# Chunk 0 of a chunked retention in whole 128-position blocks, and a new order of the early work

## The chip, the core and the metric

The kernel runs on one core of a Trainium2 chip. The core has a matrix engine (TensorE; in the profile PE for its matmuls, PEld for its weight loads), VectorE (DVE), ScalarE (ACT), GpSimd (POOL) and SyncE (SP), which issues the transfers. Each engine works through its own instructions in the order in which they were issued, and waits on semaphores for the others. Matmuls write to PSUM; DVE and ACT read it from there. The metric is the device time of one execution in microseconds.

## The reference

A retention layer with a state that decays for each head, and after it a feed-forward block with SiLU. B = 4, H = 8, S = 768, D = 64; the feed-forward block has 3072 tokens, 512 inputs and 2048 hidden units.

```python
gamma = 1.0 - 2.0 ** (-5.0 - np.arange(H))
for t in range(S):
    state = gamma * state + k[:, :, t] (outer) v[:, :, t]
    y[:, :, t] = scale * (q[:, :, t] @ state)
x = y.transpose(0, 2, 1, 3).reshape(B * S, H * D)
h = x @ w_in
out = (h * sigmoid(h)) @ w_out
```

The weights come as 64-bit floating-point words, which the kernel turns into 32-bit ones itself.

## The kernel before, in words

**Units.** The sequence is cut into 6 chunks of 128 positions. A unit n is one chunk c and one batch b, n = 4c + b, so units 0 to 3 are chunk 0 and units 4 to 7 chunk 1. Within a unit each chunk is split again into two halves of 64 positions (index o), and the 8 heads are four pairs (a) of two (j).

**Steps of a unit.** The early part of the kernel, up to line 1121, is an order written out by hand for all five engines, as calls of short functions:

- T(n), or TK(n) and TQ(n) (line 470): k and q are transposed on PE, four transposes each (line 485), and copied by ACT to kt and qt (line 486).
- K(n) scales k by its decay on DVE (line 424); KA(n) does the same on ACT in eight pieces (line 949).
- SC(n): the sums of k times v of both halves (line 514, 32 records on PE), then the scores k times q within each half (line 524, 32 records).
- A(n), three calls: the scores are masked with decay on DVE (line 532); mid, the state between the halves, is made (in chunk 0 by an ACT copy, line 538, later by a DVE addition, line 540); the state after the unit is a DVE addition (line 544).
- Q(n): q is scaled by its decay gq on DVE (line 429); in chunk 0 only the second half.
- YS(n), Y0(n), YB(n): the output, as masked scores times v (32 records, line 572), then states times q in two parts. Between the parts stands a fence: a memset on POOL (line 406) that waits for the first part, and for which the second waits.
- X(n), four calls: ACT copies the output (line 619), ACT makes its high part (line 643), DVE the rest (line 646) and the third part (line 649). The three parts of a chunk, for all four batches, are the right operand xt of the products.
- next_chunk() multiplies gq by the decay of a chunk on ACT (line 379).

**Weights.** W(i) takes slice i of w_in one step on, of eleven: two ACT passes and four DVE passes turn the words into 32-bit numbers, ACT and DVE then split these in three parts. load_w(i) issues the slice's three transfers, load(name, n) one of 256 KB.

**Products.** PP(n, i) is a third of product n (line 930; n = 16 is chunk 1, slice 0): four matmuls of 512 columns each. CL(n) closes a product: ACT copy, DVE subtraction, ACT SiLU. After the early order come pair (1, 1) and all the other products (line 744), ordered by a list, and then the second half of the feed-forward block (line 1237).

**Fillers.** fill and narrow issue matmuls of zeros into an unused or not yet written PSUM bank (lines 317 and 323). The tables FILL_T, NARROW_T, FILL_Y, NARROW_Y, FILL_FENCE and FILL_P (lines 459 to 465) say how many stand ahead of, or behind, which step.

**What sets the order.** On PE, DVE, ACT, POOL and SP the order of the early part is that of the calls; the rest of the kernel after line 1121 is ordered by hand on PE only.

Of the kernel before, what the change touches and what calls it, by code (L numbers as in the profile page):

```python
# [13 lines left out]
FP32 = mybir.dt.float32  # L14
# [20 lines left out]
def kernel(  # L35
# [39 lines left out]
    wide = moe_w_in.dtype == mybir.dt.int64  # L75

    scale = 1.0 / math.sqrt(D)
    assert math.frexp(scale)[0] == 0.5
# [95 lines left out]
    def load_w(i):  # L174
        if i >= 2 * NF:
            return
        if wide:
            t = stage.tile([128, 2 * DM], U32, tag="wf", name=f"wf_{i}")
            w_in, w_out, n = moe_w_in.bitcast(U32), moe_w_out.bitcast(U32), 256
        else:  # L180
            t = stage.tile([128, DM], FP32, tag="wf", name=f"wf_{i}")
            w_in, w_out, n = moe_w_in, moe_w_out, 128
        if i < NF:
            to = t.rearrange("p (i o f) -> o p i f", o=2, f=n)
            src = w_in[:, ts(i, n)].rearrange("(i o p) f -> o p i f", o=2, p=128)
            last[:] = [nc.sync.dma_start(out=to[0], in_=src[0]).ins]
            for j in range(2):
                nc.sync.dma_start(out=to[1, ts(j, D)], in_=src[1, ts(1 - j, D)])
        else:
            nc.sync.dma_start(out=t, in_=w_out[ts(i - NF, 128), :])  # L190
        staged[i] = t

    def convert_steps(i, out):

        t = staged.pop(i)
        if not wide:
            out.append(t)
            return
        words = t.rearrange("p (c w) -> p c w", w=2)
        lo, hi = words[:, :, 0], words[:, :, 1]  # L200
        a = conv.tile([128, DM], U32, tag="ca", name=f"ca_{i}")
        s = conv.tile([128, DM], U32, tag="cs", name=f"cs_{i}")
        r = lo if i >= NF else conv.tile([128, DM], U32, tag="cw", name=f"cw_{i}")
        with queue(evac[0] if evac else None):
            top = nc.scalar.activation(out=a.bitcast(FP32), in_=hi.bitcast(FP32), func=AF.Abs,  # L205
                                       scale=2.0 ** -3).ins
# [128 lines left out]

    lag = const.tile([128, C], FP32, tag="lag", name="lag")
    for o in range(2):
        part = lag[ts(o, D), :D]
        nc.gpsimd.iota(part, pattern=[[1, D]], base=0, channel_multiplier=-1,
                       allow_small_or_imprecise_dtypes=True)  # L340
        nc.gpsimd.affine_select(out=part, in_=part, compare_op=ALU.is_ge, fill=1.0e6,
                                base=0, pattern=[[1, D]], channel_multiplier=-1)
    decay = const.tile([128, 2, HP, D], FP32, tag="decay", name="decay")
    for j in range(2):
        for a in range(HP):
            nc.scalar.activation(out=decay[:, j, a, :], in_=lag[:, :D], func=AF.Exp,
                                 scale=float(lg[2 * a + j]))

    gk = const.tile([128, NC, H], FP32, tag="gk", name="gk")
# [8 lines left out]
    for h in range(H):  # L358
        nc.scalar.activation(out=gk[:, 0, h : h + 1], in_=pos, func=AF.Exp,
                             scale=float(-lg[h]))  # L360
        nc.gpsimd.memset(lgc[ts(h % 2, D), h // 2 : h // 2 + 1], lg[h])
    nc.gpsimd.iota(lag, pattern=[[1, C]], base=1, channel_multiplier=0,
                   allow_small_or_imprecise_dtypes=True)
    for a in range(HP):
        nc.scalar.activation(out=gq[:, a, :], in_=lag, func=AF.Exp, scale=lgc[:, a : a + 1])
# [26 lines left out]
    def banks(tag, name, n=2):  # L392
        return ps_u.tile([128, n, 512], FP32, tag=tag, name=name)
# [23 lines left out]
    def scale_k(n):  # L417
        if 0 <= n < len(units):
# [4 lines left out]
            engine = nc.gpsimd if 2 * B + 1 < n < FAR else nc.vector  # L423
            engine.tensor_tensor(out=t, in0=t, in1=g, op=ALU.mult)

    def scale_q(n):
        c, b = units[n]
        t, g = (x if c > 0 else x[:, :, D:] for x in (qt[n], gq))
        nc.vector.tensor_tensor(out=t, in0=t, in1=g, op=ALU.mult)
# [179 lines left out]
    def steps_y(n, yp):  # L609
# [5 lines left out]
        if c < LATE:  # L615
            if n == 0:
                raws.append(wpool.tile([128, LATE * B, KIN, C], FP32, tag="wq", name="ys"))
            raw = raws[0][:, n]
            nc.scalar.copy(out=raw.rearrange("p a (o t) -> p o a t", o=2), in_=yp)
# [276 lines left out]

    K, Q = scale_k, scale_q

    idle[:] = [banks("y", "idle")[:, 0]]
    narrow(idle[0], 39)  # L900
    fill(idle[0], 2)
    narrow(idle[0], 39)
    T(0), K(0)
    nc.scalar.activation(out=token, in_=lgc[:1, :1], func=AF.Silu)
    SC(0), A(0), Q(0), A(0), A(0)
    W(0), W(0), W(0), W(0), W(0)
    YA(0), YB(0), X(0)
    T(1), K(1)
    W(0)
    W(0)  # L910
    X(0), X(0)
    SC(1), A(1)
    W(0)
    A(1)
    Q(1), A(1)
    T(2), K(2)
    W(0), X(0)
    W(0), W(0)
    YA(1), SC(2)
    A(2)  # L920
    YB(1), X(1)
    A(2), Q(2), A(2)
    X(1)
    closing = {}

    made = {}
# [19 lines left out]
    def KA(n):  # L946
        t = kqv["k"][n]
        for h in range(H):
            nc.scalar.activation(out=t[:, h, :], in_=t[:, h, :], func=AF.Copy,
                                 scale=gk[:, units[n][0], h : h + 1])  # L950

    TK(3)
    TQ(3)
    K(3)
    X(1)
    X(1)
    YS(2)
    Y0(2)
    YB(2)
    X(2)  # L960
    SC(3)
    A(3)
    A(3)
    Q(3)
    A(3)
    X(2)
    W(1)
    W(1)
    X(2)
    X(2)  # L970
    YS(3)
    Y0(3)
    YB(3)
    X(3)
    X(3)
    TK(4)
    W(1)
    X(3)
    X(3)
    W(1)  # L980
    TQ(4)
    load("k",6)
    W(1)
    load_w(2)
    load("q",6)
    load("k",7)
    W(1)
    W(1)
    load("v",6)
    load("q",7)  # L990
    PP(0,0)
    KA(4)
    PP(0,1)
    W(1)
    load("k",9)
    PP(0,2)
    load("v",7)
    CL(0)
    SC(4)
    load("k",8)  # L1000
    next_chunk()
    TK(5)
    A(4)
    TQ(5)
    TK(6)
    A(4)
    Q(4)
    A(4)
    K(5)
    W(1)  # L1010
    CL(0)
    YS(4)
    load("q",8)
    W(2)
    W(2)
    W(1)
    Y0(4)
    SC(5)
    W(1)
    W(2)  # L1020
    YB(4)
    X(4)
    Q(5)
    A(5)
    CL(0)
    A(5)
    PP(1,0)
    load("q",9)
    W(2)
    W(2)  # L1030
    TQ(6)
    PP(1,1)
    W(2)
    KA(6)
    load("k",10)
    PP(1,2)
    YS(5)
    put_g(0)
    A(5)
    W(2)  # L1040
    W(2)
    Y0(5)
    W(2)
    SC(6)
    CL(1)
    CL(1)
    X(4)
    A(6)
    W(2)
    YB(5)  # L1050
    W(2)
    TK(7)
    X(4)
    A(6)
    PP(2,0)
    X(5)
    load("v",8)
    PP(2,1)
    PP(2,2)
    load("v",9)  # L1060
    A(6)
    Q(6)
    TQ(7)
    K(7)
    X(5)
    YS(6)
    load_w(3)
    CL(2)
    load("v",10)
    Y0(6)  # L1070
    SC(7)
    YB(6)
    X(6)
    load_w(4)
    A(7)
    Q(7)
    TK(8)
    TQ(8)
    A(7)
    X(6)  # L1080
    YS(7)
    Y0(7)
    CL(1)
    K(8)
    YB(7)
    A(7)
    CL(2)
    X(7)
    X(5)
    X(7)  # L1090
    TK(9)
    X(4)
    hold(masked[0])
    X(5)
    TQ(9)
    X(7)
    PP(NF,0)
    KA(9)
    SC(8)
    load("q",10)  # L1100
    X(6)
    X(7)
    X(6)
    A(8)
    put_g(0)
    next_chunk()
    PP(NF,1)
    PP(NF,2)
    CL(NF)
    load("k",11)  # L1110
    CL(2)
    CL(NF)
    A(8)
    A(8)
    CL(NF)
    put_g(0)
    Q(8)
    load("q",11)
    taken[0] = 3
    begin_w()  # L1120
    early_order.close()
    written[0] = False

# [191 lines left out]
```

## Time and profile before

| | |
|---|---|
| median of 3 runs | 611.1 us (610.76, 611.1, 611.9) |
| profiled execution | 616.74 us |
| span of it (first to last instruction) | 614.7 us |
| mean granted TensorE clock | 0.991 |
| busy: PE, PEld | 605.3 us, 499.8 us |
| busy: DVE, ACT, POOL | 396.3 us, 326.8 us, 33.4 us |
| moved by DMA | 108.89 MB, mean 177 GB/s |

How to read the rows that follow. A row of stretches has the window, its length, the busy time and the number of instructions of PE, PEld, DVE, ACT and POOL, then the granted TensorE clock, the busy share of the DMA engines and GB/s. A row of the chain of waits has its start, its length and what set the time. A row of the timeline has start, length, engine, line, operation, what it writes and reads, and in brackets the idle time before it with what ended it. A row of groups has line, engine, operation, shapes and count, then the busy time and the mean of one in ns, then idle time before. A matmul of 32-bit floats is recorded twice, once for each of its two passes, as is its weight load. The ends of matmuls are modelled.

### The profile page before, as it was taken

Reading aid. Unit: us, or ns where it says so; the run is one execution under the profiler, and the core shown is the slowest. Engines: PE = TensorE matmul, PEld = TensorE weight load, DVE = VectorE, ACT = ScalarE, POOL = GpSimd, SP = SyncE. Lnnn points to the kernel's source line nnn. Section 1 sums busy time; section 2 is a strip of 40 time slices with the busy share of each in tenths; the row PEclk is TensorE's granted clock in tenths of the full one; section 3 lists DMA queues with packets and bytes.
Section 4 is the critical chain, followed back from the end, with each engine's and each line's share of the span. In section 5 each row is a group of like instructions: output and inputs, shape, how many; then the busy total and the mean of one; then the engine's idle time right before and its main releaser. Section 6 shows DMA issues by size and latency. Waiting matters only on the chain.

```text
span 614.7 us, 13719 instructions
## 1 busy us (share of the span) xinstructions
PE 605.3 (98%) x5509; PEld 499.8 (81%) x5509; DVE 396.3 (64%) x672; ACT 326.8 (53%) x607; POOL 33.4 (5%) x89
## 2 busy tenths in 40 slices
PE   8998999999999999999999999999999999999997
PEld 6786888888888888888888888888888888888886
DVE  4885899678886667665779783735545453644632
ACT  7786877677767667776698632312221321313211
POOL 3000120100021111120000000000000000000000
PEclk9997999999999999999999999999999999999999
DMA  8995779785799699999777542523524433432301
GB/s 191 234 203 138 185 165 289 235 256 173 259 249 196 178 261 250 272 266 273 274 234 267 170 152 68 189 85 103 171 70 137 137 103 103 145 129 93 113 1 68
DMA packets 144334, 108.89 MB, mean 177 GB/s; under 512 B 101136, under 2 KB 109584, under 8 KB 144272
## 3 DMA queue, kind: packets, MB, share of 16 engines
q1 hardware_dynamic: 144272, 108.03, 62.2%
q8 instruction: 43, 0.70, 0.5%
q14 instruction: 19, 0.16, 0.1%
HBM read 66.06 MB, written 36.70 MB: 167 GB/s over the span
## 4 chain that ended last, share of the span: by engine, by line
PE 96%; ACT 1%; DMA 1%; issue 1%; SPq 1%; DVE 0%; DVEq 0%; POOL 0%; ACTq 0%; POOLq 0%
PE ha L744 28%; PE o L1237 21%; PE oa L1237 14%; PE hb L744 14%; PE ob L1237 7%; PE y L572 4%; PE sc L514 2%; PE sc L524 2%; PE ha L930 1%; DMA wf<-in_moe_w_in_dram 1%; PE kp L485 1%; PE qp L485 1%; PE hb L930 0%; PE o L1257 0%; PE kp L495 0%
## 5 line engine op out<-in xcount | busy, mean ns | idle before, releaser
L744 PE MATMUL ha<-xt,wi 128*128 128x512 f32 x736 | 184.2, 392 | 0.0
L744 PEld LDWEIGHTS ha<-xt,wi 128*128 128x128 f32 x736 | 136.7, 188 | 29.1
L1237 PE MATMUL o<-wo,gs 128*128 128x512 f32 x564 | 143.1, 389 | 0.0
L832 ACT ACTIVATE gs<-gr 128x512 fp32r<-128x512 f32 x96 | 53.2, 621 | 139.0 <-issue 137.9
L1237 PEld LDWEIGHTS o<-wo,gs 128*128 128x128 f32 x564 | 105.9, 188 | 22.0
L834 DVE TENSOR_TENSOR gs<-gr,gs 128x512 fp32r<-128x512 f32 x96 | 62.2, 686 | 94.2 <-ACT gs L832 94.2
L1237 PE MATMUL oa<-wo,gs 128*128 128x512 f32 x376 | 115.8, 389 | 0.0
L744 PE MATMUL hb<-xt,wi 128*128 128x512 f32 x368 | 98.3, 389 | 0.0
L772 DVE TENSOR_TENSOR g<-g,hb 128x512 f32<-128x512 f32 x87 | 59.6, 685 | 53.6 <-ACT g L767 39.6
L1237 PEld LDWEIGHTS oa<-wo,gs 128*128 128x128 f32 x376 | 70.6, 188 | 14.6
L744 PEld LDWEIGHTS hb<-xt,wi 128*128 128x128 f32 x368 | 69.1, 188 | 14.3
L1237 PE MATMUL ob<-wo,gs 128*128 128x512 f32 x188 | 73.1, 389 | 0.0
L777 ACT ACTIVATE g<-g 128x512 f32<-128x512 f32 x87 | 54.7, 628 | 33.2 <-DVE g L772 33.1
L767 ACT ACTIVATE g<-ha 128x512 f32<-128x512 f32 x87 | 51.7, 594 | 27.1 <-PE ha L744 18.9
L835 DVE SCALAR_TENSOR_TENSOR gs<-gs 128x512 fp32r<-128x512 f32 x96 | 62.1, 684 | 0.1
L1237 PEld LDWEIGHTS ob<-wo,gs 128*128 128x128 f32 x188 | 35.3, 188 | 7.4
L205 ACT ACTIVATE ca<-wf 128x512 f32<-128x512 f32 x32 | 21.5, 670 | 7.0 <-DVE cs L218 4.2
L532 DVE TENSOR_TENSOR am<-sc,decay 128x512 f32<-128x512 f32 x24 | 16.5, 689 | 12.2 <-PE sc L524 12.1
L1278 ACT ACTIVATE o<-o 128x512 f32<-128x512 f32 x10 | 6.0, 600 | 33.4 <-PE o L1237 33.0
L218 DVE SCALAR_TENSOR_TENSOR cs<-ca,cs 128x512 uint32<-128x512 uint32 x32 | 23.2, 724 | 0.9
L572 PE MATMUL y<-qt,mid 64*64 64x64 f32 x376 | 20.0, 224 | 2.3 <-issue 2.3
L649 DVE SCALAR_TENSOR_TENSOR xt<-xt 128x512 fp32r<-128x512 f32 x28 | 19.7, 714 | 0.6
(136 smaller groups left out, 614.0 us busy)
## 6 DMA issues: line engine op xcount, KB each, us to landing
gr<-gd SPq DMA_DIRECT2D x96, 256.0 KB, 2.7
gd<-g SPq DMA_DIRECT2D x87, 256.0 KB, 3.7
wf<-in_moe_w_out_dram SPq DMA_DIRECT2D x16, 512.0 KB, 5.0
out_dram<-o SPq DMA_DIRECT2D x23, 256.0 KB, 2.1
wf<-in_moe_w_in_dram SPq DMA_DIRECT2D x16, 256.0 KB, 4.0
wf<-in_moe_w_in_dram SPq DMA_DIRECT2D x32, 128.0 KB, 4.0
kf<-in_k_dram SPq DMA_DIRECT2D x16, 256.0 KB, 4.2
qf<-in_q_dram SPq DMA_DIRECT2D x16, 256.0 KB, 4.1
```

The lines of the kernel that those rows point to most:

```text
L205: top = nc.scalar.activation(out=a.bitcast(FP32), in_=hi.bitcast(FP32), func=AF.Abs, scale=2.0 ** -3).ins
L218: nc.vector.scalar_tensor_tensor(out=s, in0=a, scalar=3, in1=s, op0=ALU.logical_shift_left, op1=ALU.bitwise_xor)
L572: i = nc.tensor.matmul(to[ts(e, D), o, a, :], lhsT=lhsT, rhs=rhs, start=key not in started, stop=True, skip_group_check=True).ins
L649: nc.vector.scalar_tensor_tensor(out=x[2], in0=x[1].bitcast(FP32), scalar=-1.0 / EPS, in1=x[0].bitcast(FP32), op0=ALU.mult, op1=ALU.add)
L744: nc.tensor.matmul(hb if i == 2 else ha, lhsT=w_sb[f][:, i, ts(kk, 128)], rhs=xt[c][:, i, kk, :], start=kk == 0 and i != 1, stop=kk == KIN ...
L767: copied[:] = [nc.scalar.activation(out=hs, in_=ha, func=AF.Copy, scale=ONE_E).ins]
L772: taken_out[:] = [nc.vector.tensor_tensor(out=hs, in0=hs, in1=hb, op=ALU.subtract).ins]
L777: nc.scalar.activation(out=hs, in_=hs, func=AF.Silu)
L832: nc.scalar.activation(out=t[:, 0, :], in_=g, func=AF.Copy, scale=HALF)
L834: nc.vector.tensor_tensor(out=t[:, 1, :], in0=g, in1=high, op=ALU.subtract)
L835: nc.vector.scalar_tensor_tensor(out=t[:, 2, :], in0=t[:, 1, :].bitcast(FP32), scalar=-1.0 / EPS, in1=high, op0=ALU.mult, op1=ALU.add)
L1237: nc.tensor.matmul(o, lhsT=g, rhs=wo[f][:, i, :], start=f == 0 and i != 1, stop=f == NF - 1 and i != 0 or (b, f, i) == (B - 1, early_f - 1 ...
```

## The change

Units of chunk 0 are no longer split into halves. Their scores are whole blocks of 128 by 128 positions for each head (wide_scores, SW in the order); they are masked in two DVE operations of 128 by 512, one for each j (wide_mask, M); the output is the masked block times v alone (wide_out, O, in two calls), since no state comes in; the sums of k and v over all 128 positions come later (wide_sums, SU), and ACT copies them to be the state (wide_state, ST). There is no mid, no scaling of q, and no fence in chunk 0. The wide decay lies in a slot of the xt tiles; POOL copies its diagonal blocks into the old decay tile. gq is made for chunk 1 at once, so that one next_chunk() goes. KG(n) scales k on POOL. The `wide` that said in which form the weights come is now called in_words.

```diff
-    for n in range(EARLY - 2):
-        for name in "kqv":
-            load(name, n)
-        if n in (0, 3):
-            load_w(n // 3)
+    for name in "kqv":
+        load(name, 0)
+    load_w(0)
...
     decay = const.tile([128, 2, HP, D], FP32, tag="decay", name="decay")
-    for j in range(2):
-        for a in range(HP):
-            nc.scalar.activation(out=decay[:, j, a, :], in_=lag[:, :D], func=AF.Exp,
+    whole = xpool.tile([128, 3, 2, HP, C], FP32R, tag="xt", name="whole").bitcast(FP32)
+    wide_decay = whole[:, 0]
+    for a in range(HP):
+        for j in range(2):
+            nc.scalar.activation(out=wide_decay[:, j, a, :], in_=lag, func=AF.Exp,
                                  scale=float(lg[2 * a + j]))
...
-    nc.gpsimd.iota(lag, pattern=[[1, C]], base=1, channel_multiplier=0,
+    nc.gpsimd.iota(gq[:, 0, :], pattern=[[1, C]], base=C + 1, channel_multiplier=0,
                    allow_small_or_imprecise_dtypes=True)
-    for a in range(HP):
-        nc.scalar.activation(out=gq[:, a, :], in_=lag, func=AF.Exp, scale=lgc[:, a : a + 1])
+    for a in reversed(range(HP)):
+        nc.scalar.activation(out=gq[:, a, :], in_=gq[:, 0, :], func=AF.Exp,
+                             scale=lgc[:, a : a + 1])
...
+    for o in range(2):
+        nc.gpsimd.tensor_copy(out=decay[ts(o, D)], in_=wide_decay[ts(o, D), :, :, ts(o, D)])
...
+    def wide_scores(n):
+        u = banks("s", f"sc_{n}").rearrange("p j (a t) -> p j a t", a=HP)
+        ktn, qtn = kt.pop(n), qt.pop(n)
+        for a in range(HP):
+            for j in range(2):
+                nc.tensor.matmul(u[:, j, a, :], lhsT=ktn[ts(j, D), a, :],
+                                 rhs=qtn[ts(j, D), a, :], start=True, stop=True,
+                                 skip_group_check=True)
+        wide[n] = u, whole[:, 1 + n % 2]
+
+    def wide_mask(n, i):
+        u, to = wide[n]
+        masked[:] = [nc.vector.tensor_tensor(out=to[:, i], in0=u[:, i], in1=wide_decay[:, i],
+                                             op=ALU.mult).ins]
+
+    def wide_sums(n):
+        u = turn(f"su_{n}")[:, : HP * D].rearrange("p (a d) -> p a d", a=HP)
+        kf, vs = kqv["k"].pop(n), kqv["v"][n]
+        for a in range(HP):
+            for j in range(2):
+                nc.tensor.matmul(u[ts(j, D), a, :], lhsT=kf[:, 2 * a + j, :],
+                                 rhs=vs[:, 2 * a + j, :], start=True, stop=True,
+                                 skip_group_check=True)
+        wide_y[n, "sums"] = u
+
+    def wide_state(n):
+        b = units[n][1]
+        state[b] = one.tile([128, HP, D], FP32, tag="state", name=f"state_{n}", bufs=B + 2)
+        nc.scalar.copy(out=state[b], in_=wide_y.pop((n, "sums")))
+
+    def wide_out(n, i):
+        vs, am_n = kqv["v"][n], wide[n][1]
+        if i == 0:
+            wide_y[n] = banks("y", f"y_{n}")[:, 0].rearrange("p (a t) -> p a t", a=HP)
+        for a in range(HP):
+            nc.tensor.matmul(wide_y[n][ts(i ^ a % 2, D), a, :], lhsT=vs[:, 2 * a + i, :],
+                             rhs=am_n[:, i, a, :], start=True, stop=True,
+                             skip_group_check=True)
...
-    FILL_T = {2: (3, 2), 3: (0, 1)}
+    FILL_T = {1: (1, 1), 2: (1, 1), 3: (1, 1)}
     NARROW_T = {0: (8, 5)}
-    FILL_Y = {0: 1, 3: 4}
-    NARROW_Y = {0: 8}
+    FILL_Y, NARROW_Y = {}, {}
     idle = []
-    FILL_FENCE = {0: 2, 2: 2, 3: 2}
+    FILL_FENCE = {}
```

The new order of the calls up to the first product outside it, several to a line; warm() loads ACT's table for SiLU, which the old order did ahead of SC(0):

```python
TK(0) TQ(0) SW(0) M(0,0) load(k1) W(0) M(0,1) load(q1) load(v1) W(0) W(0)
load(k2) load(q2) load(v5) TK(1) O(0,0) O(0,1) K(0) W(0) TQ(1) X(0) SU(0) SW(1)
warm() M(1,0) W(0) X(0) load(k3) W(0) M(1,1) TK(2) TQ(2) O(1,0) X(0) W(0) load(q3)
O(1,1) load(v2) ST(0) X(1) load_w(1) SW(2) X(0) M(2,0) load(v3) KA(1) TK(3) W(0)
TQ(3) SU(1) M(2,1) load(k4) load(v4) O(2,0) X(1) load(k5) W(0) X(1) ST(1) W(1)
SW(3) load(q4) W(0) K(2) O(2,1) M(3,0) M(3,1) X(1) X(2) SU(2) X(2) O(3,0) ST(2)
O(3,1) load(q5) X(3) load(k6) KG(3) W(1) X(2) TK(4) X(3) KA(4) W(1) W(1) W(1)
load_w(2) SU(3) load(q6) load(k7) PP(0,0) load(v6) W(0) TQ(4) load(q7) ST(3) load(v7)
X(2) W(1) SC(4) X(3) load(q8) PP(0,1) X(3) W(1) Q(4) A(4) W(1) load(k9) A(4) PP(0,2)
A(4) CL(0) W(2) TK(5) K(5) W(1) TQ(5) TK(6) YS(4) CL(0) W(2) Y0(4) SC(5) W(2) YB(4)
load(k8) W(2) load(q9) W(1) Q(5) W(2) X(4) A(5) TQ(6) A(5) PP(1,0) X(4) W(1) PP(1,1)
YS(5) PP(1,2) CL(1) Y0(5) load_w(3) A(5) KA(6) W(2) CL(0) W(2) load(v8) SC(6) CL(1)
W(2) YB(5) W(2) W(2) load(k10) TK(7) TQ(7) A(6) X(5) PP(2,0) PP(2,1) W(2) Q(6) X(4)
put_g(0) A(6) X(5) A(6) YS(6) Y0(6) KA(7) X(5) SC(7) YB(6) X(6) TK(8) PP(2,2) CL(2)
A(7) A(7) load(v9) load(v10) TQ(8) Q(7) TK(9) CL(2) A(7) X(6) X(5) YS(7) Y0(7) YB(7)
K(8) X(7) X(7) X(4) SC(8) TQ(9) X(6) CL(2) load(q10) X(7) X(6) PP(16,0) put_g(0)
load(k11) PP(16,1) X(7) next_chunk() hold() A(8) A(8) A(8) load_w(4) PP(16,2) CL(16)
load(q11) Q(8) KA(9) CL(1) CL(16) CL(16)
```

The old order stands in the kernel's lines 903 to 923 and 952 to 1118; in it, for the steps that the prediction names: K(7) on DVE, not KA(7); KA(6) between PP(1,1) and PP(1,2), well ahead of SC(6); KA(4) behind PP(0,0), with both copies of unit 4 done; SC(4) behind PP(0,2).

More of the change, by code (lines that the diff above doesn't have):

```diff
@@ L618, in steps_y @@
             raw = raws[0][:, n]
-            nc.scalar.copy(out=raw.rearrange("p a (o t) -> p o a t", o=2), in_=yp)
+            nc.scalar.copy(out=raw if c == 0 else raw.rearrange("p a (o t) -> p o a t", o=2),
+                           in_=yp)
         elif c == LATE:
@@ L897, with SW, M, SU @@
     K, Q = scale_k, scale_q
+    def SW(n):
+        wide_scores(n)
+    def M(n, i):
+        wide_mask(n, i)
+    def SU(n):
+        wide_sums(n)
+    def ST(n):
+        wide_state(n)
+    def O(n, i):
+        wide_out(n, i)
+        if i == 1:
+            ysteps[n] = steps_y(n, wide_y.pop(n))
     idle[:] = [banks("y", "idle")[:, 0]]
@@ L902 @@
     narrow(idle[0], 39)
[L903 to L923, printed above, removed]
     closing = {}
@@ L950, in KA, with KG, warm @@
                                  scale=gk[:, units[n][0], h : h + 1])
+    def KG(n):
+        t = kqv["k"][n]
+        nc.gpsimd.tensor_tensor(out=t, in0=t, in1=gk[:, units[n][0], :].unsqueeze(2).to_broadcast(
+            [128, H, D]), op=ALU.mult)
+    def warm():
+        nc.scalar.activation(out=token, in_=lgc[:1, :1], func=AF.Silu)
+    TK(0)
+    TQ(0)
+    SW(0)
+    M(0, 0)
+    load("k",1)
+    W(0)
+    M(0, 1)
+    load("q",1)
+    load("v",1)
+    W(0)
+    W(0)
+    load("k",2)
+    load("q",2)
@@ L952 @@
+    load("v",5)
+    TK(1)
+    O(0, 0)
+    O(0, 1)
+    K(0)
+    W(0)
+    TQ(1)
+    X(0)
+    SU(0)
+    SW(1)
+    warm()
+    M(1, 0)
+    W(0)
+    X(0)
+    load("k",3)
+    W(0)
+    M(1, 1)
+    TK(2)
+    TQ(2)
+    O(1, 0)
+    X(0)
+    W(0)
+    load("q",3)
+    O(1, 1)
+    load("v",2)
+    ST(0)
+    X(1)
+    load_w(1)
+    SW(2)
+    X(0)
+    M(2, 0)
+    load("v",3)
+    KA(1)
     TK(3)
+    W(0)
     TQ(3)
-    K(3)
-    X(1)
-    X(1)
-    YS(2)
-    Y0(2)
-    YB(2)
-    X(2)
@@ L961 @@
[L961 to L965, printed above, removed]
[L966 to L993 removed]
+    SU(1)
+    M(2, 1)
+    load("k",4)
+    load("v",4)
+    O(2, 0)
+    X(1)
+    load("k",5)
+    W(0)
+    X(1)
@@ new lines @@
+    ST(1)
+    W(1)
+    SW(3)
+    load("q",4)
+    W(0)
+    K(2)
+    O(2, 1)
+    M(3, 0)
+    M(3, 1)
+    X(1)
+    X(2)
+    SU(2)
+    X(2)
+    O(3, 0)
+    ST(2)
+    O(3, 1)
+    load("q",5)
+    X(3)
+    load("k",6)
+    KG(3)
+    W(1)
+    X(2)
+    TK(4)
+    X(3)
+    KA(4)
+    W(1)
+    W(1)
+    W(1)
+    load_w(2)
+    SU(3)
+    load("q",6)
+    load("k",7)
+    PP(0, 0)
+    load("v",6)
+    W(0)
+    TQ(4)
+    load("q",7)
+    ST(3)
+    load("v",7)
+    X(2)
+    W(1)
@@ L994 @@
+    SC(4)
+    X(3)
+    load("q",8)
+    PP(0, 1)
+    X(3)
+    W(1)
+    Q(4)
+    A(4)
     W(1)
     load("k",9)
-    PP(0,2)
-    load("v",7)
+    A(4)
+    PP(0, 2)
+    A(4)
     CL(0)
-    SC(4)
-    load("k",8)
-    next_chunk()
+    W(2)
     TK(5)
-    A(4)
+    K(5)
+    W(1)
     TQ(5)
     TK(6)
[L1006 to L1010, printed above, removed]
+    YS(4)
     CL(0)
-    YS(4)
-    load("q",8)
-    W(2)
-    W(2)
-    W(1)
+    W(2)
     Y0(4)
     SC(5)
-    W(1)
     W(2)
     YB(4)
+    load("k",8)
@@ L1022 @@
+    W(2)
+    load("q",9)
+    W(1)
+    Q(5)
+    W(2)
     X(4)
-    Q(5)
     A(5)
+    TQ(6)
+    A(5)
+    PP(1, 0)
+    X(4)
+    W(1)
+    PP(1, 1)
+    YS(5)
+    PP(1, 2)
+    CL(1)
+    Y0(5)
+    load_w(3)
+    A(5)
+    KA(6)
+    W(2)
     CL(0)
-    A(5)
-    PP(1,0)
-    load("q",9)
-    W(2)
[L1030 to L1043, printed above, removed]
+    W(2)
+    load("v",8)
     SC(6)
@@ L1051 @@
     W(2)
+    W(2)
+    load("k",10)
     TK(7)
+    TQ(7)
+    A(6)
+    X(5)
+    PP(2, 0)
+    PP(2, 1)
+    W(2)
+    Q(6)
     X(4)
+    put_g(0)
     A(6)
-    PP(2,0)
     X(5)
[L1057 to L1060, printed above, removed]
-    A(6)
-    Q(6)
-    TQ(7)
-    K(7)
-    X(5)
[L1066 to L1070, printed above, removed]
+    A(6)
+    YS(6)
+    Y0(6)
+    KA(7)
+    X(5)
     SC(7)
@@ L1073 @@
     X(6)
-    load_w(4)
-    A(7)
-    Q(7)
-    TK(8)
-    TQ(8)
+    TK(8)
+    PP(2, 2)
+    CL(2)
+    A(7)
+    A(7)
+    load("v",9)
+    load("v",10)
+    TQ(8)
+    Q(7)
+    TK(9)
+    CL(2)
     A(7)
     X(6)
+    X(5)
     YS(7)
     Y0(7)
-    CL(1)
+    YB(7)
     K(8)
-    YB(7)
-    A(7)
-    CL(2)
[L1088 to L1099, printed above, removed]
+    X(7)
+    X(7)
+    X(4)
+    SC(8)
+    TQ(9)
+    X(6)
+    CL(2)
     load("q",10)
-    X(6)
     X(7)
     X(6)
-    A(8)
+    PP(NF, 0)
     put_g(0)
+    load("k",11)
+    PP(NF, 1)
+    X(7)
     next_chunk()
[L1107 to L1112, printed above, removed]
-    A(8)
-    A(8)
+    hold(masked[0])
+    A(8)
+    A(8)
+    A(8)
+    load_w(4)
+    PP(NF, 2)
     CL(NF)
-    put_g(0)
+    load("q",11)
     Q(8)
-    load("q",11)
+    KA(9)
+    CL(1)
+    CL(NF)
+    CL(NF)
     taken[0] = 3
     begin_w()
+    put_g(0)
     early_order.close()
```

20 lines of the change are left out of this document (8 added, 12 removed).

## The prediction

> **What bounds the kernel now.** First the page's busy slices, then the stretches of the first microseconds, then the chain of waits.
>
> ```profile
> span 614.7 us, 13719 instructions
> PE   8998999999999999999999999999999999999997
> PEclk9997999999999999999999999999999999999999
> DMA  8995779785799699999777542523524433432301
> 10.00:15.00 5.00, 3.76 (x78) 2.77 (x75) 3.90 (x7) 3.79 (x7) 0.00 (x0) 0.79 0.93 210
> 45.00:50.00 5.00, 2.97 (x133) 2.60 (x132) 2.71 (x5) 1.64 (x4) 0.09 (x1) 1.00 0.84 216
> 50.00:55.00 5.00, 4.70 (x78) 4.06 (x78) 3.43 (x6) 3.88 (x8) 0.09 (x1) 0.54 0.72 183
> 55.00:60.00 5.00, 5.00 (x79) 3.77 (x78) 3.19 (x5) 4.24 (x15) 0.00 (x0) 0.77 0.06 14
> ```
>
> The reader is to see two regimes. From about 60 us to the end PE is busy all the time; nothing the change touches is there, so a microsecond moved in the early order is a microsecond of the total. Before that PE waits, or runs at a lower granted clock (0.79, 0.54, 0.77). The endpoint in both kernels is the first product outside the early order (pair (1,1), line 744), and both have done the same four products, ten transposed units and nine score units by then.
>
> ```profile
> 47.31 0.23 PE y L572 x10
> 47.54 2.03 issue
> 49.57 0.34 PE y L572 x6
> 60.98 1.82 PE ha L744 x8
> q8 instruction: 43, 0.70, 0.5%
> PE 605.3 (98%) x5509; PEld 499.8 (81%) x5509; DVE 396.3 (64%) x672; ACT 326.8 (53%) x607; POOL 33.4 (5%) x89
> ```
>
> The largest single loss is a 2.03 us hole inside one stage (YB(6): 10 of its 16 matmuls before, 6 after) in which PE waited for nothing that the profile shows. PE's 11,018 instructions over 43 instruction packets are 256 each, and a pass YS, Y0, SC, YB is 48 + 64 + 16 matmuls with as many weight loads, 256 instructions, in 0.86 + 0.47 + 0.47 + 0.23 = 2.0 us (rows below), while the loads keep the queues full: I read the hole as PE out of code. Behind it the clock fell: 5 x 0.46 + 5 x 0.23 = 3.4 us of PE time lost from 50 to 60.
>
> [...]
>
> **The parts of the change, costed.** Durations are those of the profiled execution.
>
> ```profile
> 39.63 0.86 PE y L572 x48
> 40.48 0.47 PE sc L514 x32
> 40.95 0.47 PE sc L524 x32
> 37.35 0.44 PE qp L485 x4
> 41.65 0.59 PE kp L485 x4
> 63.76 0.22 PE L495 MATMUL kp<-ident,kf 64*128 64x64 f32 x1
> 63.76 0.22 PE L495 MATMUL qp<-ident,kf 64*128 64x64 f32 x1
> 63.82 0.22 PE L495 MATMUL kp<-ident,kf 64*128 64x64 f32 x1
> L532 DVE TENSOR_TENSOR am<-sc,decay 128x512 f32<-128x512 f32 x9 | 6.2, 690 | 7.4 <-PE sc L524 7.4
> L429 DVE TENSOR_TENSOR qt<-qt,gq 128x256 f32<-128x256 f32 x4 | 1.7, 416 | 0.0
> L538 ACT COPY mid<-sc 128x256 f32<-128x256 f32 x4 | 1.5, 373 | 2.5 <-DVE am L532 2.4
> ```
>
> *PE.* Four 128-column transposes take 0.44 us, 0.11 each; the small row-half matmuls start in pairs at 63.76, the next pair 0.06 later, so two row halves run at once, and 32 quarter matmuls of 64 columns in 0.47 are four at once. A whole score block is 8 matmuls (16 records) of 128 columns in two row halves: 8 x 0.11 = 0.9 us against 0.47. Sums keep their size, 0.47. The output (16 records in column halves) is 0.9 against about 0.7 for scores, mid products and fence. Unit: +0.6 us; four units +2.5. If halves didn't overlap, up to +0.9 more for scores and for output each; I take the overlap, since the quarter rows show it both ways. It is covered by waiting: from 10.66 to 26.15 PE's useful work now is some 8 us of 15.5 (three units at 0.9 + 0.94 + 0.7).
>
> *DVE and ACT, per unit of chunk 0.* Out: scaled q 0.42, state addition 0.42, mid copy 0.37. In: a second mask half 0.69 and the state copy 0.37. DVE is 0.15 lighter, ACT level. KG(3) and two copies of decay go to POOL, which has at most 0.09 us of work in the stretches quoted above.
>
> *Setup.* Eight wide decays instead of eight half ones, before the first copy on ACT:
>
> ```profile
> 2.33 1.28 ACT L346 ACTIVATE decay<-lag 128x64 f32<-128x64 f32 x8 [0.30 <-POOL lag L341]
> 4.25 1.26 ACT L365 ACTIVATE gq<-lag,lgc 128x128 f32<-128x128 f32 x4
> 5.42 0.57 ACT L486 COPY kt<-kp 128x512 f32<-128x512 f32 x1
> 10.14 0.67 ACT L205 ACTIVATE ca<-wf 128x512 f32<-128x512 f32 x1 [1.35 <-DMA wf<-in_moe_w_in_dram]
> 10.66 0.66 PE L485 MATMUL kp<-ident,kqv 128*128 128x128 f32 x4 [0.56 <-DMA kqv<-in_k_dram]
> ```
>
> Between 0.16 and 0.31 each: kt's first copy moves from 5.4 to between 5.5 and 6.4. SW(0) then ends at about 7.9, and O(0) stands behind TK(1), whose k lands at 10.66 as before (the first six loads keep their places). Hidden in full by that load; but PE is idle from 7.9 to 10.7, where before it had Y(0) and fills.
>
> *Chunk 0, 10.66 to TK(4).* I walked the order engine by engine. TK(1), O(0), TQ(1) end at 12.6; SU(0) and SW(1) wait for qt's copy (13.3) and run at a slow clock (as 10 to 15 shows now) to 15.1; SW(2) ends 18.9 (now SC(2) at 19.4); KA(1) 18.6 to 20.6 delays kt and qt of unit 3, so SW(3) ends at 23.1; DVE's K(2) and masks set O(3) at 25.7. TK(4) then starts at 25.7 against 26.15: **-0.4 us**. Loads moved around it (v2, v3 later, v5 and w1 earlier) keep 5 us from issue to landing in the walk; the tightest is q of unit 4, due at 28.4 and there at about 28.5.
>
> ```profile
> 26.15 0.66 PE L485 MATMUL kp<-ident,kqv 128*128 128x128 f32 x4
> 28.93 2.02 ACT L949 ACTIVATE kqv<-kqv,gk 128x64 f32<-128x64 f32 x8
> 27.85 1.26 SPq L188 DMA_DIRECT2D wf<-in_moe_w_in_dram  x2
> 34.44 0.68 ACT L205 ACTIVATE ca<-wf 128x512 f32<-128x512 f32 x1
> 35.99 0.23 PE y L572 x16
> 41.42 0.23 PE y L572 x16
> L379 ACT ACTIVATE gq<-gq,step 128x128 f32<-128x128 f32 x8 | 2.5, 388 | 0.0
> 42.22 0.69 DVE L532 TENSOR_TENSOR am<-sc,decay 128x512 f32<-128x512 f32 x1
> 42.82 0.68 DVE L129 SCALAR_TENSOR_TENSOR wi<-wi,wil 128x512 fp32r<-128x512 f32 x1
> ```
>
> *To YB(4).* One next_chunk goes (1.3 us of ACT). But KA(4), 2.0 us, now stands ahead of qt's copy for unit 4, so SC(4) waits until 30.6 and two thirds of product 0 come after it; and slice 2's first step, which stands ahead of kt and qt of unit 5 on ACT, waits for w2. Its last issue ends at 29.1 and, with 5 us to land as slice 0 had, it is there at 34.0. Both together: YB(4) ends at 36.4 against 36.2, **+0.6** from TK(4).
>
> *KA(6) and KA(7).* Each is 2.0 us of ACT directly ahead of the SC that needs it, with two copies of X before it on the same queue. SC(6) waits from 40.3 to 41.5, YB(5) ends 42.7 against 41.65: **+0.8**. SC(7) waits from 46.3 to 47.95, YB(6) ends at 49.1, against 47.4 had the old kernel had no hole; a third of product 2 is still to come. **+1.6**, of which the end takes back 1.3: there DVE's last X steps (one start every 0.60 us, 42.22 to 42.82) bound both kernels. By the same walk the old order without its hole reaches pair (1,1) at 55.8; the new one at 57.1. So the order as such costs -0.4 + 0.6 + 0.8 + 1.6 - 1.3 = **+1.3 us**.
>
> *The hole.* It and its slow clock are 60.6 - 55.8 = **-4.8 us**. Chunk 0 issues 64 fewer matmuls per unit, so 512 PE instructions, two blocks, fewer; the block boundary no longer falls there, and the dense pass itself is now cut by the wait for KA(7), which gives code time to arrive. Bounds: -4.8 if no hole comes, 0 if one of the same size comes elsewhere.
>
> *Fills.* All fences' and outputs' fills go, those ahead of transposes become one each.
>
> ```profile
> L317 PE MATMUL y<-zero 128*128 128x512 bf16 x5 | 1.4, 383 | 0.0
> ```
>
> In themselves they cover waits. What goes is their hold on the clock. The 2.03 us hole was enough to lower it, so the waits of 2.8 us (7.9 to 10.7), 1.2 us (SC(6)) and 1.65 us (SC(7)) may be too. A slow stretch as now after 12.9 is some 3.4 us, up to 1.7 us of PE time. Bounds 0 and 5.1; since much of what follows waits for DVE or ACT anyhow I take one part in four, **+1.3**.
>
> [...]
>
> *Shapes.* The four transposes behind YB(5) take 0.59 us (41.65), those between two parts of a product 0.44: 0.15 us for a change of matmul shape. The new order has about two more changes a unit in chunk 0, 1.2 us in all; I take 0, as PE waits around them, and keep 1.2 as the upper bound.
>
> Sum: +1.3 - 4.8 + 1.3 = -2.2 us; that makes 616.74 into 614.5 for a profiled execution, whose span is 614.7 and has 2.0 around it. It is 5.6 above the median, 611.1; if the hole is in all runs, the median becomes **608.9 us**.
>
> **Rivals.** (1) *No hole and no added slow clock*, with DVE and ACT starting a little faster than walked: -3.5 to -5, some 607. For it: DVE starts each 0.60 where records say 0.69. Against: the fills go. (2) *The hole stays*, by another block boundary in a dense pass, or it was never in the timed runs: the 5.6 us between profile and median are close to its 4.8. Then +1.3 + 1.3: 613.7, slower. Against: three timed runs show no scatter of that size. (3) *The clock decides*: with PE idle from 7.9 to 10.7 the rate falls before TK(1), O(0), TQ(1), and again behind SC(6) and SC(7). Three stretches, 3 x 1.7 = 5.1: 1.3 - 4.8 + 5.1 = +1.6, 612.7; it decides from the second stretch on. (4) *Changes of shape eat it*: eight at 0.15 on the path, -2.2 + 1.2 = -1.0, 610.1, no change that can be told. For it: the row at 41.65. Against: in chunk 0 PE waits for copies and masks. [...] That the whole does nothing, since loads set the pace (DMA slices of 9 until 50 us), is in the same chance: 611.1; against it, PE's longest wait for a load is 0.56 us.
>
> **Chances.** Forecast 0.42, (1) 0.14, (2) 0.26, (3) 0.12, (4) 0.06. Less than 0.2% (1.2 us) can't be told from no change. Faster: 0.36 of the forecast's 0.42 and all of (1), 0.50. Within: 0.05 + 0.01 + 0.02 + 0.04 = 0.12. Slower: 0.01 + 0.25 + 0.10 + 0.02 = 0.38. The range reaches to (1)'s far side, 606, with 0.5 for the walk's own error, and to the slower cases at 613.7 with 1.1 more: 605.5 to 614.8. The forecast alone: 607 to 610.5.
>
> **What would show it.** No gap of 2 us in PE's rows before pair (1,1); PE's first L744 row near 58.4; TK(4) near 25.7; SC(6) and SC(7) waiting for L949; a granted clock under 1 in one stretch of 3.4 us more or less. It is wrong if a hole of PE's sequencer appears elsewhere, if whole-block stages take 1.8 us instead of 0.9, or if a slow clock reigns through 10 to 20 us.

## The result, and the profile after

| | before | after |
|---|---|---|
| median | 611.41 us (7 runs, 610.76 to 613.72) | 615.79 us (7 runs, 614.39 to 618.79) |
| ratio to before, 95% interval | | 1.0073 (1.0050 to 1.0096) |
| profiled execution, its span | 616.74 us, 614.7 us | 615.79 us, 614.0 us |

The new kernel is slower by 4.4 us, although its profiled execution is shorter than the one of before that the prediction was made on. That profile lies above all seven timed runs of the old kernel; the profile of after is right at its median.

Lines of the page of after:

```profile
span 614.0 us, 13160 instructions
PEclk9999999999999999999999999999999999999999
```

Stretches of after (window, length, busy time and count of PE, PEld, DVE, ACT, POOL, clock, DMA share, GB/s):

```profile
10.00:15.00 5.00, 4.42 (x41) 3.41 (x41) 2.40 (x5) 2.32 (x4) 0.00 (x0) 1.00 1.03 221
45.00:50.00 5.00, 4.95 (x136) 4.00 (x135) 3.15 (x7) 3.79 (x13) 0.09 (x1) 1.00 1.01 208
50.00:55.00 5.00, 4.70 (x144) 3.91 (x142) 4.71 (x9) 4.17 (x8) 0.09 (x1) 1.00 0.33 70
55.00:60.00 5.00, 4.18 (x25) 3.40 (x21) 4.17 (x9) 3.66 (x11) 0.00 (x0) 1.00 0.83 210
```

No hole at 47 us and no lowered clock behind it, as forecast. The chain of waits of after:

```profile
15.61 1.28 ACT L996
...
28.29 1.91 ACT kqv L987 x8
...
40.42 1.91 ACT kqv L987 x8
...
46.87 0.48 ACT kqv L987 x2
47.35 0.03 issue
47.38 1.72 PE sc L555 x29
...
55.09 0.77 issue
...
59.71 1.81 PE ha L786 x8
```

Four things are to be seen: the load of ACT's table for SiLU (L996, warm), which lay at 6.89 in the profile of before, under the wait for k, is now part of the chain; the scaling of k on ACT (L987, KA) stands in the chain ahead of SC(4), SC(6) and SC(7); a new hole of 0.77 us stands between SC(8) and TQ(9); and the endpoint, the first product of line 786, comes at 59.7 in the chain, where the profiled execution of before had it at 60.98.

The timeline of after, PE:

```profile
7.04 2.08 PE L434 MATMUL sc<-qt,kt 64*128 64x128 f32 x16 [0.54 <-ACT qt L527]
...
11.62 1.98 PE L464 MATMUL y<-whole,kqv 128*64 128x128 f32 x16
...
15.16 1.16 PE L434 MATMUL sc<-qt,kt 64*128 64x128 f32 x16
...
17.66 1.09 PE L464 MATMUL y<-whole,kqv 128*64 128x128 f32 x16
...
26.48 0.66 PE L526 MATMUL kp<-ident,kqv 128*128 128x128 f32 x4
```

The first whole-block stages take 2.08 and 1.98 us, the next of the same kind 1.16 and 1.09: in this execution PE ran at half rate until about 14 us. Its clock records begin at 13.8 us only, and the views print 1.00 ahead of that, so the durations have to be read, not the digit. The second profile of this kernel, below, is different there.

### The profile page after: what moved, and what is told of

It reads as the page before. It is cut to its first block, busy times and chain, and to the rows that moved or that the text cites. A ratio compares the mean times of both kernels' runs of the same rounds, so it can differ in the third digit from the quotient of the medians.

```text
span 614.0 us, 13160 instructions
## 1 busy us (share of the span) xinstructions
PE 604.6 (98%) x5234; PEld 499.4 (81%) x5234; DVE 392.4 (64%) x665; ACT 329.4 (54%) x619; POOL 34.6 (6%) x86
## 4 chain that ended last, share of the span: by engine, by line
PE 94%; ACT 3%; DMA 1%; SPq 1%; DVE 0%; issue 0%; POOL 0%; DVEq 0%; POOLq 0%
PE ha L786 28%; PE o L1342 21%; PE oa L1342 14%; PE hb L786 14%; PE ob L1342 7%; PE y L613 3%; PE sc L555 2%; PE sc L565 1%; ACT kqv L987 1%; DMA kqv<-in_k_dram 1%; PE ha L968 1%; PE kp L526 1%; PE y L464 1%; PE qp L526 0%; PE hb L968 0%; PE o L1362 0%
## 5 line engine op out<-in xcount | busy, mean ns | idle before, releaser
L1384 DVE TENSOR_TENSOR o<-o,o 128x512 f32<-128x512 f32 x10 | 6.8, 688 | 19.3 <-ACT o L1383 19.3
L573 DVE TENSOR_TENSOR am<-sc,decay 128x512 f32<-128x512 f32 x20 | 13.7, 686 | 6.3 <-PE sc L565 6.3
```

## The experiments

Theory A: the hole of 2 us and the slow clock behind it belong to the one profiled execution of before. Theory K: the three ACT scalings ahead of their SC cost the time. Theory C: chunk 0 and its slow clock do. Theory F, formed from the gaps: PE's unexplained holes stand where a block of 256 instructions ends and the next one is late. Theory O: the new order costs it, not the whole blocks. Each ratio is to the kernel before, run beside it; it is an estimate with a 95% interval, not the quotient of the two medians. Before's median was 612.95 to 613.57 us in these series.

### The kernel before again, two more profiles

No edit.

> The kernel before, unchanged, for a second profile. If the hole of 2 us at 47.5 us belongs to the one profiled execution alone (theory A), this profile has no gap of PE's of 1 us or more between 45 and 52 us, its first L744 row is at 55 to 56 us, and its span is some 609 us. If the hole is in every execution (theory B), it is there again, the first L744 row is at 60 to 61, and the 4.4 us by which the new kernel is slower have to come from elsewhere than its early order.

> The kernel before once more. If the hole of 2.25 us with a halved clock behind it is usual: a gap of 2 us or more at instruction 2241 and a clock under 1 after 50 us. If the first profile was a rare one: a gap of 0.5 to 1.5 us there, no lower clock after 50 us, the first L744 row at 55 to 57 us.

Chain of waits of the second profile, then its stretch of 50 to 55 us, then the chain of the third:

```profile
47.40 1.18 issue
...
57.27 1.81 PE ha L744 x8
```

```profile
50.00:55.00 5.00, 4.70 (x139) 3.61 (x142) 5.00 (x10) 4.97 (x14) 0.09 (x1) 1.00 0.91 241
```

```profile
48.76 0.36 issue
...
57.80 1.82 PE ha L744 x8
```

The hole is at the same place in all three, inside YB(6), but 2.03, 1.18 and 0.36 us long in the chain, and the clock stays full behind the shorter ones (1.00 from 50 to 55 us, against 0.54). The endpoint comes at 57.3 and 57.8, not 60.98; the spans are 612.1 and 611.6 against 614.7. Neither expectation of the second profile was met as it stood (theory A wanted no gap of 1 us and an endpoint of 55 to 56, theory B the same hole again); what holds of theory A is that most of the 4.8 us belongs to the first profile: place fixed, length a matter of the execution. Between endpoint and end of the span all three take 553.9 to 555.0 us, and the two profiles of the new kernel 554.3 and 554.4, so in these profiles the difference lies ahead of the endpoint.

### The new kernel again

No edit.

> The new kernel, unchanged, beside the others. Ratio to before 1.004 to 1.008 as at first. Theory F (PE's holes stand where an instruction block of 256 ends and the next one, asked for a block earlier, is late behind the loads): any gap of 0.5 us or more that no engine explains stands at instruction 256k - 64 of PE, here again near 1985 (SC(8) to TQ(9)).

616.87 us, ratio 1.0056 (1.0037 to 1.0076); again a gap of 0.77 us in the chain between SC(8) and TQ(9). The start is another one. Timeline of its PE, then its stretch of 10 to 15 us:

```profile
6.81 1.16 PE L434 MATMUL sc<-qt,kt 64*128 64x128 f32 x16 [0.80 <-ACT qt L527]
...
10.65 0.90 PE L526 MATMUL kp<-ident,kqv 128*128 128x128 f32 x4 [2.37 <-DMA kqv<-in_k_dram]
11.48 1.98 PE L464 MATMUL y<-whole,kqv 128*64 128x128 f32 x16
```

```profile
10.00:15.00 5.00, 4.35 (x39) 3.32 (x40) 2.06 (x4) 2.13 (x4) 0.00 (x0) 0.66 0.90 205
```

SW(0) runs at full rate (1.16 us); then PE waits 2.37 us for k, and behind that wait the granted clock is 0.50 from 10.9 to 14.3 us, so that O(0) takes 1.98. The endpoint comes at 59.81, against 59.54.

### Scaling k of units 4, 6, 7 on POOL

```diff
-    KA(4)
+    KG(4)
-    KA(6)
+    KG(6)
-    KA(7)
+    KG(7)
```

> The new kernel with k of units 4, 6 and 7 scaled on POOL (KG in KA's three places), nothing else changed. Theory K (the three ACT scalings right ahead of their SC cost the time): SC(4), SC(6) and SC(7) no longer wait for ACT; 2 to 3 us faster than the new kernel, 612.8 to 613.8, ratio to before 1.002 to 1.004. Theory C (chunk 0 and its slow clock cost it): less than 1 us faster, 615 or more, ratio over 1.005.

616.02 us, ratio 1.0041 (1.0011 to 1.0070), a little above what theory K expected and not told apart from the new kernel. In its chain the hole behind SC(8) has grown, from 0.77 us:

```profile
53.62 1.66 issue
```

### Keeping PE busy around SW(0)

```diff
+    narrow(idle[0], 20)
     SW(0)
+    narrow(idle[0], 60)
```

> The new kernel with 20 matmuls of zeros of 32 columns ahead of SW(0) and 60 behind it. Theory C: PE runs at the full clock from about 10 us instead of 14, O(0) takes 1.1 us instead of 2.0, TK(4) comes 1 to 1.8 us earlier and the time falls by 1 to 1.8 us, to about 614.3, ratio 1.005. Theory K: the gain is eaten by ACT, whose queue sets the pace from 14 us on; under 0.5 us, ratio 1.007.

618.5 us, ratio 1.0082 (1.0046 to 1.0117): no gain. Timeline of its PE, then its chain:

```profile
7.16 1.16 PE L434 MATMUL sc<-qt,kt 64*128 64x128 f32 x16
8.26 1.67 PE L323 MATMUL idle<-zero 128*128 128x32 bf16 x60
...
10.91 1.09 PE L464 MATMUL y<-whole,kqv 128*64 128x128 f32 x16
```

```profile
36.13 1.27 issue
...
43.54 1.26 issue
...
188.48 1.68 issue
```

PE ran at full rate from SW(0) on and TK(4) came at 25.58 instead of 26.48, just short of theory C's 1 us. But 80 matmuls are 160 instructions, every block ends 160 instructions earlier in the work, and two holes of 1.3 us appear where the new kernel has none. This is what led to theory F. The third hole lies far behind the early order, and the granted clock falls to 0.50 behind it (191.1 to 194.5 us). The endpoint is at 60.38, 0.8 us behind the new kernel's; from there to the end it takes 3.5 us longer (558.0 us).

### The new chunk 0, then the old order; with and without a warm PE

The order up to TK(4) is the new one, behind it the old one (K(7) on DVE, KA(6) between the thirds of product 1, PP(0) ahead of SC(4)). The second kernel also has PE busy around SW(0), with 70 small matmuls taken from the start so that the count stays:

```diff
-    narrow(idle[0], 39)
-    fill(idle[0], 2)
-    narrow(idle[0], 39)
+    fill(idle[0], 7)
+    narrow(idle[0], 3)
...
+    narrow(idle[0], 16)
     SW(0)
+    narrow(idle[0], 54)
```

> The new kernel's order up to TK(4), then the old order (with one next_chunk, and SU(3) and ST(3) put in); so the old places of the scalings of k, with KA(6) early and K(7) on DVE. Theory K: most of the loss is behind TK(4), so this is 2.5 to 4 us faster than the new kernel, 612 to 613.3, ratio 1.001 to 1.003. Theory C: the loss stays in chunk 0, 615 or more, ratio over 1.005.

> The order with the new chunk 0 and the old order behind TK(4) (ratio 1.0016 at first), with PE kept busy ahead of and behind SW(0) by 70 small matmuls that are taken from the start, so that the number of instructions, and with it every block boundary, stays. Theory C in the part that is left: the clock is full from about 10 us, TK(4) comes about 1 us earlier, 0.5 to 1.2 us faster than that kernel, ratio 0.999 to 1.001. If the clock early on doesn't matter: ratio 1.0016 again.

614.17 us, ratio 1.0016 (1.0001 to 1.0032), and 613.84 us, ratio 1.0012 (0.9992 to 1.0032). The old order behind TK(4) takes back most of the loss, with as many PE instructions as in the new kernel (5234 matmuls). What the clock of the first 14 us costs isn't told apart from nothing.

### Whole blocks in the old order

The new functions for chunk 0 with the old loads, fills and places of all steps, and one next_chunk(). Against the new kernel, the first of many lines of this kind:

```diff
-    TK(0)
-    TQ(0)
-    SW(0)
-    M(0, 0)
-    load("k",1)
...
+    T(0), K(0)
...
+    SW(0), M(0, 0), M(0, 1), SU(0), ST(0)
+    W(0), W(0), W(0), W(0), W(0)
+    O(0, 0), O(0, 1), X(0)
+    T(1), K(1)
```

> The whole blocks alone, in the old order: the old loads, the old fills, the old places of every step (SU, ST in the old places of sums and state), one next_chunk. If the blocks themselves cost the time (PE's 2.5 us more), 613.5 to 615, ratio 1.002 to 1.006. If the new order costs it (theory O), the old order hides them: 610 to 612.5, ratio 0.997 to 1.001, since two block boundaries and one next_chunk go.

613.63 us, ratio 1.0004 (0.9977 to 1.0031). The whole blocks cost nothing that can be told (the interval leaves room for up to 1.9 us): theory O. Its chain shows a hole at the end of YB(6), this time inside TK(8), since the blocks of instructions end elsewhere (its gap is at instruction 1729, not 2241):

```profile
46.61 0.26 PE kp L532
46.87 0.83 issue
47.70 0.55 PE kp L532 x3
```

### The kernel before with four loads later

v of units 9 and 10 and slices 3 and 4 of w_in are issued behind SC(8), the first of them like this:

```diff
-    load("v",9)
...
     SC(8)
...
+    load("v",9)
```

> The kernel before with four loads (v of units 9 and 10, slices 3 and 4 of w_in) moved behind SC(8), ahead of q of unit 10. Theory F: with fewer loads in the queues the instruction block asked for at 44 us arrives in time, no gap over 0.5 us at instruction 2241, the first L744 row near 55, 1 to 2 us faster than before, ratio 0.997 to 0.999. If the hole has nothing to do with the loads: same hole, ratio 1.000, or slower where a load is late.

613.76 us, ratio 1.0006 (0.9987 to 1.0026). The gap at instruction 2241 was 0.57 us in its profile, as in the third profile of the kernel before, where no load was moved (0.58), and the first L744 row came at 55.75, but the time didn't fall: a miss for the expected ratio.

### Moving every block boundary in the new kernel

```diff
-    fill(idle[0], 2)
-    narrow(idle[0], 39)
+    fill(idle[0], 3)
+    narrow(idle[0], 23)
```

> The new kernel with 16 small matmuls of the first warm-up replaced by one long one: 30 instructions fewer before any work, so every block boundary of PE falls 30 instructions later in the work; the one between SC(8) and TQ(9) (gap of 1.0 us in two profiles) then falls within the products behind it. Theory F: the gap goes, the first L744-like row comes 0.8 to 1 us earlier, the time falls by 0.8 to 1 us, ratio 1.0045 to 1.006. If the gap is a wait of that place in the program and not of the block: it stays, ratio unchanged.

> The same shift with k of units 4, 6 and 7 scaled on POOL. In the first such kernel the boundary's gap had grown to 1.9 us and eaten part of the gain. Theory K with F: both losses gone, 2 to 3.5 us faster than the new kernel, ratio 1.001 to 1.003. Theory K wrong: no faster than after_shift.

616.3 us, ratio 1.0046 (1.0028 to 1.0064), and with scaling on POOL 614.39 us, ratio 1.0016 (0.9998 to 1.0033). Timeline of PE of the first:

```profile
54.52 0.66 PE L526 MATMUL qp<-ident,qf 128*128 128x128 f32 x4
55.01 0.60 PE L317 MATMUL ha<-zero 128*128 128x512 bf16 x2
55.26 2.19 PE L968 MATMUL ha<-xt,wi 128*128 128x512 f32 x8
```

The hole between SC(8) and TQ(9) is gone, and the product behind it starts at 55.26 instead of 56.60; 0.46 of that stands at TK(4) already, which came at 26.02. Timeline of PE of the second, and its POOL group:

```profile
41.07 0.65 PE L555 MATMUL sc<-kqv 64*64 64x64 f32 x32
...
46.48 0.69 PE L555 MATMUL sc<-kqv 64*64 64x64 f32 x32
...
56.99 1.98 PE L786 MATMUL ha<-xt,wi 128*128 128x512 f32 x8
```

```profile
L992 POOL TENSOR_TENSOR kqv<-kqv,gk 128x512 f32<-128x512 f32 x4 | 4.5, 1122 | 19.8 <-PE kp L526 19.8
```

SC(7)'s first part is one run of 0.69 us at 46.48, where after has 1.72 us from 47.38 as the eight pieces of KA(7) arrive. Between these two kernels only the engine that scales k differs: 0.30%, some 1.8 us (0.05 to 0.55% by their two intervals). In their profiles the endpoint moves by 1.2 us, from 58.19 to 56.99, and SC(4), SC(6) and SC(7) wait less. How much of it is these waits, and how much that the rest of ACT's queue moves forward too, isn't told apart. The step from the new kernel to the shifted one, 0.10 to 0.27% by its two series, lies within the intervals; that the hole went is shown by the profile alone.

### Trying to beat both

Against whole blocks in the old order, for k of units 4 to 8, and for the two shifts, the fills at the start:

```diff
-    KA(4)
+    KG(4)
...
-    K(5)
+    KG(5)
...
-    narrow(idle[0], 39)
-    fill(idle[0], 2)
-    narrow(idle[0], 39)
+    fill(idle[0], 8)
+    narrow(idle[0], 13)
```

> Whole blocks in the old order, with k of units 4 to 8 scaled on POOL instead of ACT and DVE. PE's waits for k at SC(4) and SC(5) (0.4 us at 34 us) go and DVE is 1.8 us lighter: 0.5 to 1.5 us faster than before, ratio 0.9975 to 0.999. Against it: POOL's 1.13 us stands ahead of the fences' memsets, and a dense pass that runs without waits makes the next block's hole longer; then ratio 1.000 or above.

> The same with the four loads (v of units 9 and 10, slices 3 and 4) behind SC(8). Theory F: the hole behind YB(6) (1.16 us at instruction 1729) falls under 0.5 us, 0.5 to 1 us faster than whole_pool, ratio 0.996 to 0.998. If the loads behind don't matter, the same ratio as whole_pool.

> Whole blocks in the old order, k scaled on POOL, every block boundary 118 instructions later in the work. The gap of 1.7 us behind YB(6) moves into YS(7) to YB(7), where PE waits for the fence anyway, and falls under 0.8 us: 0.5 to 1.2 us faster than whole_pool, ratio 0.997 to 0.999. If the gap only moves: ratio 0.9995 again.

> The kernel before with the first warm-up made of 21 instead of 80 matmuls, 118 instructions fewer, so each block boundary falls 118 instructions later in the work. If the hole costs the timed executions 4 us or more (as the prediction had it): 3 us or more faster, ratio 0.995. If it costs them 1 to 1.5 us, with DVE's X steps bounding the end anyway: 0 to 1.2 us faster, ratio 0.998 to 1.000. If another boundary takes its place: 1.000 or above, with a gap of over 0.5 us at another multiple of 256 less 64.

Whole blocks in the old order with k of units 4 to 8 on POOL: 613.26 us, ratio 0.9995 (0.9977 to 1.0013), above the 0.9975 to 0.999 that were expected; with the four loads later 613.71 us, 1.0000 (0.9976 to 1.0024); the gap behind YB(6) was 1.71 us in both profiles, so the part of theory F that blames the loads missed a second time. With every boundary 118 instructions later in the work: 616.28 us, ratio 1.0050 (1.0030 to 1.0071), and the same shift made to the kernel before 616.08 us, ratio 1.0043 (1.0026 to 1.0060). Chain of the shifted whole-block kernel, then of the shifted kernel before:

```profile
34.27 0.66 issue
...
40.43 1.28 issue
...
51.06 0.50 issue
...
185.71 1.86 issue
187.56 0.34 PE y L619 x6
187.90 3.54 PE ha L792 x8
```

```profile
34.67 0.50 issue
...
49.10 1.11 issue
...
184.81 1.93 issue
```

In the whole-block kernel the gap behind YB(6) went and one of 0.72 us stands in YS(7) to YB(7), as expected; but holes opened elsewhere, and the expected gain missed. For the kernel before the third case that was expected came true: slower, with a gap over 0.5 us at another multiple. The longest holes are the last ones, at 185 us, in a stage far behind the early order. In the whole-block kernel the granted clock then falls to 0.51 (188 to 191.5 us), and eight matmuls take 3.54 us where 1.81 is usual. There most of the loss lies: the endpoint of the shifted kernel before is at 56.83, earlier than in the three profiles without the shift, but 556.2 us follow instead of 553.9 to 555.0; with whole blocks the endpoint moves by 1.0 us and what follows by 3.6 (555.0 to 558.6). No version beat the kernel before. Taking out 118 filler instructions, ahead of any work, cost more than half of what the change that was studied cost.

### Where the holes stand

Counted in the traces: PE's instructions (weight loads, matmuls and PE's semaphore instructions) up to each unexplained gap, from one start to the next, and the 16 KB packets of the instruction queue.

```
kernel            gap us  at instruction      previous boundary, packet starts, lands, PE resumes
before            2.24    2241 = 256*9 - 63   44.26  47.07  48.01  49.57
before, second    1.40    2241                43.90  46.15  47.19  48.58
before, third     0.58    2241                45.36  46.59  47.66  49.12
after             1.03    1985 = 256*8 - 63   52.21  53.34  54.30  55.87
pool_scale        1.92    1985
warm_fill         1.49    1217 = 256*5 - 63   30.79  34.53  35.85  37.4
whole_old_order   1.16    1729 = 256*7 - 63
before_shift      2.14    5313 = 256*21 - 63  179.57 184.08 185.34 186.74
whole_pool_shift  2.07    4801 = 256*19 - 63  181.94 184.88 186.14 187.56
```

"Previous boundary" is the time at which PE passed the boundary one block before. From there to the start of the packet it took 1.1 to 4.5 us, then 0.9 to 1.3 us to land, and 1.4 to 1.6 us more until PE went on: 3.7 to 7.2 us. In the rows with times PE had work for 2.6 to 5.1 us between the two boundaries, and what is left, 0.58 to 2.24 us, is the hole. That PE asks for a block at the boundary one block before it is the author's reading and isn't shown. Counted are the places, 256k - 63 for every gap in this table, and the packets: in the profiles of before and after exactly one starts behind each such boundary of the first 60 us, ten and eight in all, 0.4 to 2.7 us after the first instruction behind the boundary. In the three profiles of before the hole is the longer, the later the packet starts (2.8, 2.3 and 1.2 us). That the loads in the queues make it late isn't shown: moving four of them left the gap at 1.71 us in one kernel and at 0.57 in the other, where 0.58 was seen without, and the new kernel's own hole came with a packet that started after 1.1 us, in a stretch (50 to 55 us) where the DMA engines were busy for 0.33.

## Why the prediction was wrong

**The step that failed** is the hole, "60.6 - 55.8 = -4.8 us", with the condition "if the hole is in all runs". It is in all three profiles of the kernel before, but 0.36 to 2.03 us long, and the granted clock fell behind the longest alone (0.50 from 50.4 to 57.3 us). The usual endpoint of the kernel before is at 57.1 to 57.6 us (first rows of line 744 in the second and third profiles), not at 60.6 (the first profile's row is at 60.8). So the saving was 3.0 to 3.5 us too large: there were 1.3 to 1.8 us to win, and the new order brought a hole of its own (0.77 us in the chain of both its profiles), which the prediction named as what would make it wrong. The 5.6 us between profile and median, which rival 2 names, were the sign that the profile was no usual execution. Rival 2 had the mechanism; its sum of +2.6 us fits the profiles, whose endpoints differ by 1.9 to 2.7 us, while its 613.7 us is 2.1 under the median.

**The endpoint of the new kernel** was forecast near 58.4 and came at 59.54 and 59.81: the walk was 1.1 to 1.4 us short, of which 0.77 is the new hole.

**TK(4)** was forecast at 25.7, measured 26.48 and 26.74. The walk had the slow clock from 12.9 us. In the first profile PE was at half rate until about 14 (SW(0) took 2.08 us, 1.16 in the second), in the second from 10.9 to 14.3; in both O(0) took 2.0 us, and qt's second copy came at 14.5 in the first, instead of 12.7. In the three profiles of before TK(4) was at 26.15, 24.58 and 27.36. That is rival 3's place; what it costs the time stays open, since the warm kernel with an unchanged count was 1.0012 against 1.0016.

**Whole blocks** were put at 0.9 us a stage and took 1.0 to 1.1 from start to start at the full clock (rows of 1.1 to 1.2). Right in kind, up to 0.2 short; the halves do run side by side, and whole blocks in the old order cost nothing that can be told.

**KA(6) and KA(7)** were right in kind: SC(6) forecast for 41.5, measured 41.75; YB(6)'s end forecast for 49.1, measured 49.87. That SC(6) came so near is partly luck, since TK(4) was 0.8 late and the walk from there 0.5 too long. Their net price was put at 1.1 us, with up to 0.6 more for KA(4); the 1.8 us of scaling on POOL (0.05 to 0.55%) don't contradict that. The order behind TK(4) as a whole was put at +1.7; the new order up to TK(4) with the old one behind it was 0.40 to 0.57% faster than the new kernel, 2.5 to 3.5 us, with intervals of 1 us and more to either side, so this term may be too small.

**The table load of ACT** (1.28 us, and 0.20 for the instruction behind it) was left out of the walk: it was hidden under k's load before and stands in the chain at 15.61 now. No run moved it alone, so its price is open.

**The slow clock** behind the waits, +1.3, was right in kind for one wait of the three: in the second profile of after the clock is 0.50 for 3.4 us behind the 2.37 us that PE waits for k, and it stays full behind SC(6) and SC(7) (1.00 from 13.8 us on in the first). But two of the three profiles of before have such a stretch as well (12.9 to 16.3 and 13.6 to 17.0 us), so no run shows that it made the new kernel slower.

**The moved loads** and the change of shape played no part that a run showed.

**The sum that the runs support**, as ratios: new kernel 1.0056 to 1.0073; without its hole 1.0046; without the ACT scalings too 1.0016; with the old order throughout instead 1.0004. The first and the last of these steps are within their intervals. In the profiles the endpoints differ by some 2 us, the times by 3.4 to 4.4; where the rest lies isn't known.

## What to carry to other kernels

A saving that is one long hole in one profile should be priced from several executions: look whether the place is fixed and how the length varies. A step on a busy queue right ahead of its consumer can delay it, so scale early or on the engine that has nothing to do; but the price is to be measured, since three scalings of 2.0 us each cost 1.8 us together here. Where a stage issues hundreds of small instructions, count them in blocks of 256: adding or removing fillers moves every later boundary, and 118 instructions fewer brought holes of 1.86 and 1.93 us here, at 185 us, in a stage far from the edit.

## What the runs showed of the hardware that was not expected

The change from one block of instructions to the next isn't hidden here: holes of 0.4 to 2 us (1.86 and 1.93 at 185 us) at the counts of the table, 256k - 63, with lengths that differ from one execution to the next. 118 instructions fewer at the start made two kernels slower, to 1.0043 and from 0.9995 to 1.0050. The granted clock reads 1.00 before the first change that the records hold (13.8 us in the first profile of after), while PE's durations (2.08 against 1.16 us for the same 16 matmuls) show half rate.
